# SyncE's first transfer becomes a small spare DMA transpose, and the x rows come as one transfer from ScalarE's queue

## The chip, the cores and the metric

The kernel runs on one core of a Trainium2 chip. The metric is the device time of one execution in microseconds. Before the change six executions gave a median of 272.99 us (272.6 to 274.35); at prediction time three of them were known, with a median of 272.78. A profile's span leaves out about 2 us at the ends (271.2 of 273.31 us in the profiled run before), so spans and times are not mixed below.

## The reference

```python
def reference(x, w_gate, w_up, w_down):          # x: 32 x 32 x 1024, bf16
    return (_gelu(x @ w_gate) * (x @ w_up)) @ w_down   # F = 3584, gelu by tanh
```

## The kernel before

A recorded program: each engine has its list of operations, and waits are worked out from the tiles that they share. Every transfer has a semaphore, and equal places in the schedule keep the order of the source. What matters here is the start. TensorE runs eight matmuls on constants, whose results are not used, transposes the first two column blocks of x itself, and the other blocks of x come by DMA transpose.

```python
        one = nc.const_aps.tensor(1.0, [P, 512], BF16)
        ...                                        # GpSimd builds the identity matrix
        for n in [512] * 6 + [P] * 2:
            mm(3, one[:, 0:P], one[:, 0:n], True, True)

        NX = 2
        for i, eng in enumerate(("sp", "act")):    # x rows, two halves, one on each queue
            dma(eng, xn[:, 2 * i:2 * i + 2, :], x_r[:, 2 * i:2 * i + 2, 0:NX * P], 0, f"xn{i}")

        def load_first(eng, j, k0, k1, after=()):  # j = 0: w_gate, 1: w_up
            dma(eng, first[:, j, k0:k1, :], w_r[j][:, k0:k1, 0:4 * P], 0, f"w0_{j}_{k0}", after)

        def load_x(h, k0, k1, after=()):
            pr.add("sp", "dma_start_transpose", xT[h][:, k0:k1, :], xf[h * 512:(h + 1) * 512, k0 * P:k1 * P],
                   dma=f"x{k0}_{h}", after=after)

        for k in range(NX):
            load_first("sp", 0, k, k + 1)
            load_first("act", 1, k, k + 1)
        for k0, k1 in ((2, 3), (3, 4), (4, 5), (5, 6), (6, 8)):
            load_x(0, k0, k1)
        for k in range(2, 4):
            load_first("act", 0, k, k + 1)
            load_first("act", 1, k, k + 1)
        act(warm[:, 0:1], const0, GELU, 0)
        for k in range(NX):
            for i, b in enumerate((6, 7) if k == 0 else (4, 5)):
                half = ps[:, b, 0:P].bitcast(BF16)
                for t in range(2):
                    pr.add("pe", "transpose", half[:, t * P:(t + 1) * P],
                           xn[:, 2 * i + t, k * P:(k + 1) * P], ident[:, :])
                pr.add("dve", "tensor_copy", xT[0][:, k, i * 256:(i + 1) * 256], half)
        ...
        # the first real matmuls: for k, for j (gate, up), for m in 0..3
        op = mm(2 * m + j, first[:, j, k, m * P:(m + 1) * P], xT[0][:, k, :], ...)
```

So the first real matmul needs three things: TensorE's transposes of the x rows, DVE's copies of them, and the first w_gate block. The destination tile of real matmuls is `arena` in the profile (`first` and `xT` lie in it); `xn` lies in `hT`.

Of the kernel before, what the change touches and what calls it, by code (L numbers as in the profile page):

```python
# [6 lines left out]
P = 128  # L7
# [116 lines left out]
def bass_standalone__geglu_ffn__sampling_kernel(  # L124
# [7 lines left out]
    xf = x.flatten_outer_dims()  # L132
# [3 lines left out]
    DK, FM = D // P, F // P  # L136
# [3 lines left out]
    x_r = xf.rearrange("(tc p) d -> p tc d", p=P)  # L140
# [3 lines left out]
    pr = _Program()  # L144

    with ExitStack() as es:
        def sb(name, shape, dtype):
            return es.enter_context(nc.sbuf_tensor(name, shape, dtype))

        hT = sb("hT", [P, FM, N], BF16)  # L150
# [15 lines left out]
        xn = hT[:, FM - 1, :].rearrange("p (t c) -> p t c", c=2 * P)  # L166
# [22 lines left out]
        def dma(eng, out, a, at, name, after=()):  # L189
            return pr.add(eng, "dma_start", out, a, at=at, dma=name, after=after)  # L190
# [10 lines left out]
            mm(3, one[:, 0:P], one[:, 0:n], True, True)  # L201

        NX = 2
        for i, eng in enumerate(("sp", "act")):
            dma(eng, xn[:, 2 * i:2 * i + 2, :], x_r[:, 2 * i:2 * i + 2, 0:NX * P], 0, f"xn{i}")

        def load_first(eng, j, k0, k1, after=()):
            dma(eng, first[:, j, k0:k1, :], w_r[j][:, k0:k1, 0:4 * P], 0, f"w0_{j}_{k0}", after)
# [414 lines left out]
```

## Time and profile before

| | before |
|---|---|
| median time | 272.99 us (6 runs, 272.6 to 274.35) |
| span of the profiled run | 271.2 us |
| TensorE busy | 267.6 us, 99% |
| x rows landed | 3.23 and 3.40 us |
| first w_gate block: issued, landed | 1.26, 4.25 us |
| first real matmul | 4.61 us |
| TensorE at full speed from | 6.3 us |

All places are microseconds from the start of the span. TensorE alone is the bound, so a later first matmul is paid at the end. The lines themselves are in the prediction below. Two of its habits are used throughout: start plus time to landing gives the landing, and the distance of two weight loads for 512 columns tells TensorE's speed: 0.43 us up to 6.3 us in this trace, called half speed below, and 0.216 us after it, called full speed.

### The profile page before, as it was taken

What the parts mean: (1) busy time and instruction counts of PE and PEld (TensorE: products, weight loads), DVE (VectorE), ACT (ScalarE), POOL (GpSimd) and SP (SyncE); (2) the same over time, 40 slices, a digit from 0 to 9 for tenths busy, and PEclk for the clock granted to TensorE, in tenths of its full rate; (3) what the DMA queues carried; (4) which work ended last, traced back from release to release, by engine and by line L of the source; (5) the groups of instructions that cost most, each with busy time, mean ns of one, the idle gap of its engine ahead of it and who ended that gap; (6) DMA issues with size and microseconds to landing.
All of it is one profiled execution on the core that took longest, in us unless ns stands there. A gap on an engine that the chain in (4) does not pass through costs nothing.

```text
span 271.2 us, 3314 instructions
## 1 busy us (share of the span) xinstructions
PE 267.6 (99%) x1197; PEld 191.8 (71%) x1206; DVE 203.5 (75%) x238; ACT 132.8 (49%) x213; POOL 37.2 (14%) x23
## 2 busy tenths in 40 slices
PE   8999999999999999999999999999999999999996
PEld 4444448888888888888776776664458888888884
DVE  1341998998899889988764739289976999999911
ACT  2335776566756675667455564531220305067452
POOL 1000003023302330234345060000000000000000
PEclk9999999999999999999999999999999999999999
DMA  7999960050492500942900070293010000002102
GB/s 189 275 282 186 276 187 4 9 147 0 120 294 53 155 0 2 282 145 65 248 0 0 0 259 14 81 347 117 0 39 19 4 0 0 0 0 80 58 19 97
DMA packets 47039, 27.46 MB, mean 101 GB/s; under 512 B 8624, under 2 KB 47024, under 8 KB 47024
## 3 DMA queue, kind: packets, MB, share of 16 engines
q1 hardware_dynamic: 44800, 25.30, 34.4%
q10 hardware_dynamic: 2224, 1.97, 2.8%
q8 instruction: 9, 0.15, 0.2%
q14 instruction: 6, 0.05, 0.1%
HBM read 23.33 MB, written 2.10 MB: 94 GB/s over the span
## 4 chain that ended last, share of the span: by engine, by line
PE 99%; issue 0%; DVE 0%
PE ps L117 99%; DVE o L117 0%
## 5 line engine op out<-in xcount | busy, mean ns | idle before, releaser
L117 PE MATMUL ps<-S,T 128*128 128x512 f32 x560 | 129.2, 391 | 0.0
L117 PEld LDWEIGHTS ps<-S,T 128*128 128x128 f32 x560 | 105.1, 188 | 22.5
L117 ACT ACTIVATE tmp<-ps 128x512 f32<-128x512 f32 x64 | 38.0, 595 | 52.2 <-PE ps L117 52.2
L117 POOL TENSOR_TENSOR T<-arena 128x1024 fp32r<-128x1024 bf16 x17 | 36.5, 2156 | 124.4 <-PE ps L117 74.2
L117 PE MATMUL ps<-T,S 128*128 128x512 f32 x224 | 51.3, 390 | 0.0
L117 DVE TENSOR_TENSOR T<-arena,T 128x1024 fp32r<-128x1024 bf16 x42 | 50.9, 1218 | 0.2
L117 PEld LDWEIGHTS ps<-T,S 128*128 128x128 f32 x224 | 42.0, 188 | 8.8
L117 DVE TENSOR_TENSOR hT<-tmp,ps 128x512 bf16<-128x512 f32 x56 | 37.2, 684 | 14.3 <-PE ps L117 11.9
L117 ACT ACTIVATE ps<-ps 128x512 f32<-128x512 f32 x44 | 25.6, 583 | 36.6 <-PE ps L117 36.6
L117 PE MATMUL ps<-arena 128*128 128x512 bf16 x186 | 42.6, 384 | 0.4
L117 DVE TENSOR_TENSOR tmp<-ps,tmp 128x512 f32<-128x512 f32 x28 | 19.4, 692 | 23.2 <-PE ps L117 23.2
L117 PEld LDWEIGHTS ps<-arena 128*128 128x128 bf16 x192 | 17.8, 98 | 24.3 <-issue 3.2
L117 DVE TENSOR_TENSOR T<-arena 128x1024 fp32r<-128x1024 bf16 x25 | 30.0, 1220 | 5.0 <-PE ps L117 4.3
L117 DVE TENSOR_TENSOR ps<-ps,tmp 128x512 f32<-128x512 f32 x32 | 22.2, 695 | 3.0 <-PE ps L117 3.0
L117 PE MATMUL ps<-arena,hT 128*128 128x512 bf16 (+2 forms) x124 | 24.3, 355 | 0.1
L117 PEld LDWEIGHTS ps<-arena,hT 128*128 128x128 bf16 x126 | 11.7, 98 | 12.7 <-issue 0.5
L117 ACT ACTIVATE tmp<-tmp 128x512 f32<-128x512 f32 x28 | 17.6, 633 | 2.4 <-DVE tmp L117 2.1
L117 DVE TENSOR_TENSOR S<-hT 128x1024 fp32r<-128x1024 bf16 x14 | 16.6, 1219 | 0.0
L117 ACT ACTIVATE T<-arena 128x1024 fp32r<-128x1024 bf16 x14 | 14.8, 1059 | 0.0
L117 ACT ACTIVATE ps<-hT 128x512 f32<-128x512 f32 x18 | 10.7, 599 | 8.0 <-DVE hT L117 8.0
L117 ACT ACTIVATE hT<-ps 128x512 f32<-128x512 f32 x14 | 8.0, 599 | 10.8 <-PE ps L117 10.8
L117 PE MATMUL ps<-S 128*128 128x512 f32 x56 | 12.9, 389 | 0.0
(32 smaller groups left out, 89.1 us busy)
## 6 DMA issues: line engine op xcount, KB each, us to landing
arena<-in_w_down_dram SPq DMA_DIRECT2D x4, 1792.0 KB, 8.8
arena<-in_w_gate_dram SPq DMA_DIRECT2D x10, 512.0 KB, 4.0
arena<-in_w_up_dram SPq DMA_DIRECT2D x10, 512.0 KB, 5.4
out_dram<-arena SPq DMA_DIRECT2D x12, 128.0 KB, 1.7
arena<-in_w_gate_dram SPq DMA_DIRECT2D x4, 256.0 KB, 5.0
arena<-in_w_up_dram SPq DMA_DIRECT2D x4, 256.0 KB, 5.1
arena<-in_w_up_dram ACTq DMA_DIRECT2D x4, 128.0 KB, 4.0
arena<-in_w_gate_dram ACTq DMA_DIRECT2D x2, 256.0 KB, 4.0
```

The source lines that it names most:

```text
L117: ins = name(eng, *args, **kw) if callable(name) else getattr(eng, name)(*args, **kw)
```

## The change

Nothing states the intent. My reading is that the spare transpose was to pay for whatever a first DMA transpose costs before it matters, and that the x rows then had to leave SyncE's queue. The spare's destination is a piece of hT that is written over much later; its data are never used.

```diff
         NX = 2
-        for i, eng in enumerate(("sp", "act")):
-            dma(eng, xn[:, 2 * i:2 * i + 2, :], x_r[:, 2 * i:2 * i + 2, 0:NX * P], 0, f"xn{i}")
+        pr.add("sp", "dma_start_transpose", hT[:, FM - 2, 0:P], xf[0:P, 0:P], dma="spare")
+        dma("act", xn[:, :, :], x_r[:, 0:4, 0:NX * P], 0, "xn")
```

## The prediction

> **What bounds the kernel now.** I read the busy totals first, then the chain of work that ended last, then the timeline of the first 14 us, because the diff touches only the first transfers of two queues, and last the DMA rates of that stretch in half microseconds.
>
> The page's busy totals and its chain:
>
> ```profile
> PE 267.6 (99%) x1197; PEld 191.8 (71%) x1206; DVE 203.5 (75%) x238; ACT 132.8 (49%) x213; POOL 37.2 (14%) x23
> ...
> PE 99%; issue 0%; DVE 0%
> PE ps L117 99%; DVE o L117 0%
> ```
>
> TensorE is the bound from the first microsecond to the last, and nothing else carries more than a trace of the chain. The chain in order of time shows the one place that this change can reach:
>
> ```profile
> 0.73 0.04 issue
> 0.77 3.79 PE ps L117 x16
> 4.56 0.05 issue
> 4.61 8.11 PE ps L117 x33
> 12.72 0.05 issue
> ```
>
> Sixteen TensorE instructions run before 4.56 us: eight matmuls on constants that do no useful work, then eight transposes of x rows. The real stream begins at **4.61** and does not stop again for longer than 0.07 us. So a later start moves the end; an earlier landing of anything else buys nothing.
>
> The timeline (start, length, engine, operation, count, idle time before it and its releaser):
>
> ```profile
> 0.73 0.48 ACTq L117 DMA_DIRECT2D hT<-in_x_dram  x1
> ...
> 0.74 0.46 SPq L117 DMA_DIRECT2D hT<-in_x_dram  x1
> ...
> 0.77 2.93 PE L117 MATMUL ps<-const-bfloat16-1.0 128*128 128x512 bf16 x8 [0.77 <-PEq L608]
> ...
> 1.26 0.92 SPq L117 DMA_DIRECT2D arena<-in_w_gate_dram  x2
> ...
> 2.23 6.75 SPq L117 DMA_TRANSPOSE arena<-in_x_dram  x5
> ...
> 3.50 1.06 PE L117 MATMUL ps<-ident,hT 128*128 128x128 bf16 x8
> ...
> 3.96 0.93 DVE L117 COPY arena<-ps 128x256 bf16<-128x256 bf16 x4 [3.96 <-PE ps L117]
> ...
> 4.58 0.14 PEld L117 LDWEIGHTS ps<-arena 128*128 128x128 bf16 x2 [0.28 <-DMA arena<-in_w_gate_dram]
> 4.61 9.62 PE L117 MATMUL ps<-arena 128*128 128x512 bf16 x39
> 4.99 0.15 PEld L117 LDWEIGHTS ps<-arena 128*128 128x128 bf16 x1 [0.28 <-DVE arena L117]
> ...
> 5.84 0.15 PEld L117 LDWEIGHTS ps<-arena 128*128 128x128 bf16 x1 [0.28 <-issue]
> 6.27 7.25 PEld L117 LDWEIGHTS ps<-arena 128*128 128x128 bf16 x34 [0.28 <-issue]
> ```
>
> Three things are to be seen. The two halves of the x rows leave at 0.73 and 0.74; the answers on DMA issues give 2.7 and 2.5 us to landing, so 3.4 and 3.2. The transposes start at 3.50, just behind the constant matmuls, so those cover the wait. The first real matmul needs the DVE copies of the first column block (the second of the four ends near 4.46) and the first w_gate block (issued 1.26, landing 3.0 us later, 4.26). Both come together; that is the tuned start. Then the weight loads are 0.43 us apart up to 6.27, and afterwards 34 take 7.25 us, 0.216 apart: TensorE runs at half speed up to about 6.3 us.
>
> [...] 0.43 us then 0.216 us per matmul, the change at 6.3 us, 5.5 us after the first matmul. [...] with both queues filled, the rate is 283 to 326 GB/s and no higher:
>
> ```profile
> 1.50:2.00 0.50, 0.50 (x2) 0.15 (x1) 0.00 (x0) 0.00 (x0) 0.00 (x0) 1.00 0.13 41
> 2.00:2.50 0.50, 0.50 (x3) 0.22 (x2) 0.00 (x0) 0.00 (x0) 0.00 (x0) 1.00 0.95 283
> ...
> 3.00:3.50 0.50, 0.50 (x5) 0.23 (x3) 0.00 (x0) 0.00 (x0) 0.00 (x0) 1.00 1.09 317
> ```
>
> (The last two columns are the DMA engines' busy share and GB/s.) [...]
>
> **The change, part by part.**
>
> *Removed:* one 128 KB transfer from SyncE's queue (0.46 us of issue) and one wait of TensorE, since one semaphore now stands for both halves.
>
> *Moved:* ScalarE's first transfer carries 256 KB in place of 128. Its issue stays near 0.5 us: a later ordinary load of four 512-byte runs per partition took 0.51. First data came close to 1.9 us (41 GB/s in the half microsecond to 2.0, about 20 KB, under 0.1 us of full rate). 256 KB at 300 GB/s is 0.87 us, so the last byte is on its way at about 2.8. Before, the two halves shared the engines and held the same bytes: the same 2.8, then landings of 3.2 and 3.4. The gap from last byte to landing stays, so I expect **3.3 to 3.5** and transposes from 3.50 to 3.6. The third transpose waited for the second half; now the first waits for all, with 0.1 us less slack. Cost: 0 to 0.1 us.
>
> *Added:* one DMA transpose of one 128x128 block (32 KB). Of five transposes on this queue, the four of four blocks took 1.21 to 1.26 us of issue and the one of eight took 1.59. That is (1.59 - 1.26) / 4 = 0.08 us a block, so one block should take 1.26 - 3 x 0.08 = **1.0 us** of issue, an estimate from those rows. Its 32 KB are 0.1 us of the engines at 300 GB/s. Its destination, a piece of hT, is not used before 18 us.
>
> *Pushed back:* the first w_gate block leaves at about 0.74 + 1.0 + 0.05 = 1.8 instead of 1.26. Transfers issued at that place (1.76, 1.80) took 3.4 and 3.6 us to landing with both queues full; the one issued at 1.26 took 3.0. SyncE's queue now has 128 KB fewer in front of it and ScalarE's 128 KB more, so I take 3.1: landing at **4.9** instead of 4.26. The first real matmul, at 4.61, then starts near 4.9 to 5.0, 0.35 us later.
>
> *What this costs at the end:* while TensorE is at half speed, 0.35 us of delay is 0.35 / 0.43 = 0.8 matmul not done before 6.3 us. They are done later at 0.216 us each: 0.8 x 0.216 = **0.18 us**, provided that full speed still comes at 6.3.
>
> *What does not bite:* everything else on SyncE's queue is about 0.5 us later. Eight matmuls use one row block of x. With full speed from 6.27, the 17th matmul (block 2) starts at 6.27 + 12 x 0.216 = 8.9, the 25th at 10.6, the 33rd at 12.3. The transposed x blocks landed at 2.23 + 5.3 = 7.5, 3.48 + 6.1 = 9.6 and 4.78 + 5.0 = 9.8. The slacks are 1.4, 1.0 and 2.5 us, all over 0.5. The second w_gate block lands near 5.7 and is wanted at 7.1.
>
> Sum: +0.1 to +0.3 us on the middle case.
>
> **The rivals.**
>
> *A, the clock comes later.* TensorE's idle gap before the real stream grows from 0.25 us (4.36 to 4.61) to about 0.6. [...] For it: the three times before, 272.6, 272.78 and 274.35, already spread by 1.75[...]. [...] I give it about 15 to 20%; time 274 to 275.
>
> *B, the first transpose is dear.* The first of the five needed 5.3 us to landing although its issue was no longer than the others'. If a transpose holds up the ordinary transfers behind it on the same queue, w_gate lands at 5.5 to 6 and the start moves by 1 to 1.4 us, half of which counts at low clock: +0.5 to +0.7, and more of rival A. Against it: ordinary loads followed the later transposes (issued from 25.73) with a landing in 4.9 us, which is no worse than elsewhere. Time 273.5 to 274.5.
>
> *C, hidden or a small gain.* If w_gate lands by 4.5, the copies still set 4.61 and nothing moves: 272.8. A gain would need an earlier 4.61, and the copies stand in the way: constant matmuls until 3.5, transposes, copies, none of them shorter. A spare transpose that made the later ones faster would help blocks that already have 1.0 us of slack or more. So a gain beyond run-to-run luck is nearly excluded.
>
> **Range and chances.** The middle case is 272.78 + 0.2 = 273.0; with rivals A and B at their weights I put **273.1**. The low end, 272.4, is the best run before less its own scatter[...]. Two per cent is 5.5 us, more than the whole start-up stretch could lose short of a stall of the transposes: faster 0.01, same 0.97, slower 0.02.
>
> **What the changed profile would show.** Right: a first SyncE issue of about 1.0 us, w_gate's first issue at about 1.8 with some 3.1 us to landing, transposes on TensorE at 3.5 to 3.6, the first matmul on arena at 4.9 to 5.0 with the w_gate transfer as its releaser, matmul spacing changing at 6 to 7 us, and the chain after it unbroken as before. Wrong: an issue of the spare over 1.5 us, an arena matmul after 5.3, the spacing of 0.43 lasting past 8 us, or matmuls on blocks 2 and 3 that wait for an x transpose. If the x rows land after 3.8, the single transfer is the dearer part and my working of it failed.

## The result

The changed kernel is correct and takes **276.27 us** (median of 6 runs, 274.35 to 277.73) against 272.99. The ratio is 1.0107 (95% interval 1.0064 to 1.0150): slower by about 1.1%, inside the 2% that counts as the same, but outside the predicted 272.4 to 274.7. Ratios here and below are the mean time of one kernel's fast runs over that of the other's of the same rounds, so not quite the ratio of the medians.

The profiled run is the slowest of the six, 277.73 us with a span of 275.4; four of the others have spans of 274.0 and one of 272.0. So the profile shows the worst case, and its 4.2 us are more than the mean loss of about 3.

The busy totals and the chain on the page of the changed kernel:

```profile
PE 269.6 (98%) x1197; PEld 192.2 (70%) x1206; DVE 203.4 (74%) x238; ACT 132.8 (48%) x213; POOL 37.1 (13%) x23
...
PE ps L117 96%; DMA arena<-in_w_gate_dram 2%; SPq L117 0%; DVE o L117 0%
```

A DMA has come into the chain that was TensorE from end to end. Its beginning in order of time (start, length, what):

```profile
0.74 1.22 SPq L117
1.96 0.06 issue
2.02 4.94 DMA arena<-in_w_gate_dram
6.96 0.05 issue
7.01 9.92 PE ps L117 x33
```

The issue of the spare transpose takes 1.22 us of SyncE's queue, then the w_gate block needs **4.94 us** from issue to landing, and only then the real matmuls begin: 7.01 us instead of 4.61. The timeline tells what TensorE did meanwhile and afterwards:

```profile
0.73 0.42 ACTq L117 DMA_DIRECT2D hT<-in_x_dram  x1
...
3.77 0.77 PEld L117 LDWEIGHTS ps<-ident,hT 128*128 128x128 bf16 x8 [0.33 <-DMA hT<-in_x_dram]
...
7.00 0.13 PEld L117 LDWEIGHTS ps<-arena 128*128 128x128 bf16 x2 [2.47 <-DMA arena<-in_w_gate_dram]
...
12.10 0.15 PEld L117 LDWEIGHTS ps<-arena 128*128 128x128 bf16 x1 [0.28 <-issue]
12.45 5.28 PEld L117 LDWEIGHTS ps<-arena 128*128 128x128 bf16 x25 [0.20 <-issue]
```

The x rows came at 3.72, 0.3 us later than before; that is hidden behind w_gate. TensorE then stood still from 4.80 to 7.01. Its weight loads stay 0.43 us apart until 12.1: full speed comes at about 12.3 us, before it came at 6.3. The two losses add up to the whole. The start moved by 7.01 - 4.61 = 2.40 us. Half-speed work after the start lasts 12.3 - 7.01 = 5.3 us instead of 6.3 - 4.61 = 1.7, and each microsecond of it loses half (0.43 us a matmul against 0.216): (5.3 - 1.7) / 2 = 1.8. Together 4.2, and the spans differ by 275.4 - 271.2 = 4.2.

The DMA rates of the changed kernel (last column GB/s, before it the DMA engines' busy share):

```profile
3.00:3.50 0.50, 0.50 (x4) 0.17 (x2) 0.00 (x0) 0.00 (x0) 0.00 (x0) 1.00 1.14 326
3.50:4.00 0.50, 0.44 (x5) 0.23 (x4) 0.00 (x0) 0.00 (x0) 0.00 (x0) 1.00 0.94 74
4.00:4.50 0.50, 0.50 (x8) 0.50 (x6) 0.30 (x2) 0.16 (x1) 0.00 (x0) 1.00 0.33 41
4.50:5.00 0.50, 0.31 (x3) 0.04 (x1) 0.50 (x3) 0.50 (x1) 0.00 (x0) 1.00 0.68 133
5.00:5.50 0.50, 0.00 (x0) 0.00 (x0) 0.13 (x1) 0.50 (x1) 0.00 (x0) 1.00 0.99 301
```

The same two half microseconds from 3.5 in the kernel before:

```profile
3.50:4.00 0.50, 0.50 (x7) 0.50 (x6) 0.04 (x1) 0.00 (x0) 0.00 (x0) 1.00 0.93 279
4.00:4.50 0.50, 0.50 (x6) 0.29 (x3) 0.50 (x3) 0.27 (x1) 0.00 (x0) 1.00 0.96 326
```

Before, they moved 279 and 326 GB/s; here they move 74 and 41. ScalarE's queue is hit too: single packets of its second w_up block (issued at 1.74, 5.04 us to landing) are recorded with 0.71 to 0.98 us, where 0.046 is usual. The dip begins soon after the spare's last data packets (3.33) and outlasts its landing (4.39) a little. Theories to test: the spare transpose makes the dip; the merged rows do; the queue position does; and the idle gap, not the delay, costs the clock.

### The profile page after: what moved, and what is told of

It reads as the page before. It is cut to its first block, busy times and chain, and to the rows that moved or that the text cites.

```text
span 275.4 us, 3315 instructions
## 1 busy us (share of the span) xinstructions
PE 269.6 (98%) x1197; PEld 192.2 (70%) x1206; DVE 203.4 (74%) x238; ACT 132.8 (48%) x213; POOL 37.1 (13%) x23
## 4 chain that ended last, share of the span: by engine, by line
PE 96%; DMA 2%; SPq 0%; issue 0%; DVE 0%
PE ps L117 96%; DMA arena<-in_w_gate_dram 2%; SPq L117 0%; DVE o L117 0%
## 5 line engine op out<-in xcount | busy, mean ns | idle before, releaser
L117 PE MATMUL ps<-arena 128*128 128x512 bf16 x186 | 44.4, 396 | 2.6 <-DMA arena<-in_w_gate_dram 2.2
```

Of the source, the lines that this page charges most:

```text
L117: ins = name(eng, *args, **kw) if callable(name) else getattr(eng, name)(*args, **kw)
```

## The experiments

Twelve kernels ran. Apart from one that is wrong, all were correct. "Start" is the first real matmul.

### Taking the parts apart: merge_only, spare_plain, spare_halves

`merge_only` has the merged rows alone:

```diff
-        pr.add("sp", "dma_start_transpose", hT[:, FM - 2, 0:P], xf[0:P, 0:P], dma="spare")
         dma("act", xn[:, :, :], x_r[:, 0:4, 0:NX * P], 0, "xn")
```

> The x rows as one ScalarE transfer, no spare transpose: SyncE's first transfer is the w_gate block. Theory T (the spare transpose stalls the DMA engines for about 1 us after its packets): w_gate issued at 0.74, landing by 3.7; x rows landing at 3.3 to 3.7; first matmul on arena at 4.6 to 4.9; no half microsecond below 150 GB/s between 3.0 and 5.0 us; time 272.5 to 273.5. Rival M (the merged x transfer is what delays the start): x rows land at 3.7 or later and w_gate's landing after 5, first arena matmul after 5.5, time 275 or more.

Measured: ratio 1.0068 (1.0045 to 1.0091), median 274.87. My theory expected 273 and missed. w_gate landed at 3.58, but the rows at 4.47, and they now begin the chain:

```profile
0.74 3.73 DMA hT<-in_x_dram
4.47 0.04 issue
4.51 1.04 PE ps L117 x8
5.55 0.05 issue
5.60 9.01 PE ps L117 x33
```

In the packet records SyncE's w_gate packets begin at 1.8 us and the rows' packets only at 2.7; with the spare in front, the rows began at 1.8. Nearly no data move from 2.0 to 2.5 (45 GB/s), and no transpose has a packet by then. So this move has a cost of its own, and a dip can come without a transpose.

`spare_plain` keeps the changed order but makes the spare an ordinary transfer of the same block:

```diff
-        pr.add("sp", "dma_start_transpose", hT[:, FM - 2, 0:P], xf[0:P, 0:P], dma="spare")
+        dma("sp", hT[:, FM - 2, 0:P], xf[0:P, 0:P], 0, "spare")
```

> The changed kernel with the spare as an ordinary transfer of the same 128x128 block, same place and bytes. Theory T (it is the transposing that stalls): issue near 0.5 us, w_gate issued at about 1.3 and landing near 4.3, first arena matmul 4.6 to 5.0, no half microsecond under 150 GB/s from 3.0 to 5.0, time 272.7 to 273.7. Rival Q (anything in front of w_gate on SyncE's queue, with 256 KB in front on ScalarE's, delays it so): w_gate lands after 6, dip in the DMA rate between 3.5 and 4.5, time about 276.

Measured: ratio 1.0020 (0.9986 to 1.0055), median 273.54. Issue of the spare 0.40 us, w_gate issued at 1.21 and landed 3.09 us later, at 4.30; the rows at 3.94, start 5.07. Its DMA rates:

```profile
3.50:4.00 0.50, 0.22 (x3) 0.01 (x1) 0.00 (x0) 0.00 (x0) 0.00 (x0) 1.00 1.11 381
4.00:4.50 0.50, 0.50 (x6) 0.50 (x7) 0.08 (x1) 0.00 (x0) 0.00 (x0) 1.00 1.25 325
```

Where the transpose gave 74 and 41, the ordinary transfer gives 381 and 325. The start is 0.1 us late of the expected range, the rest is as the theory said. So here it is the transposing that delays w_gate (4.94 us to landing against 3.09), not the place in the queue. Its longer issue (1.22 us against 0.40) belongs to it: w_gate left 0.8 us earlier here, so this run does not part the issue from what follows it.

`spare_halves` adds the spare to the kernel before, between SyncE's half of the rows and w_gate:

```diff
             dma(eng, xn[:, 2 * i:2 * i + 2, :], x_r[:, 2 * i:2 * i + 2, 0:NX * P], 0, f"xn{i}")
+        pr.add("sp", "dma_start_transpose", hT[:, FM - 2, 0:P], xf[0:P, 0:P], dma="spare")
```

> The kernel before with only the spare transpose added, between SyncE's half of the x rows and w_gate. The x rows should land as before, 3.2 to 3.5. If the spare ahead of w_gate is the cause by itself: w_gate issued near 2.5, landing 6 to 7.3, first arena matmul after 6, time 275 to 277. If the spare hurts only together with the merged rows: w_gate lands before 5.5, first arena matmul before 5.6, time 273 to 274.

Measured: ratio 1.0110 (1.0064 to 1.0155), median 275.52. Rows at 3.40 and 3.59; the start at 6.56 follows w_gate, as expected of the spare as the cause by itself:

```profile
1.25 1.19 SPq L117
2.44 0.06 issue
2.50 4.01 DMA arena<-in_w_gate_dram
```

The spare alone costs as much as the whole change. The merged rows alone cost 0.7%, and on top of the spare nothing, because w_gate is later than the rows then. The two delays lie side by side and did not add: 1.0110 and 1.0068 alone, 1.0107 together.

### What the idle gap costs: after_fill, merge_fill

`after_fill` is the changed kernel with TensorE kept busy while it waits:

```diff
                 pr.add("dve", "tensor_copy", xT[0][:, k, i * 256:(i + 1) * 256], half)
+        for n in range(5):
+            mm(3, one[:, 0:P], one[:, :], True, True)
```

> The changed kernel with five more 512-column constant matmuls (5 x 0.43 = 2.1 us) between the transposes and the first arena matmul, so that TensorE is not idle from 4.8 to 7.0. Theory H (of the 4.2 us lost in the profile, 2.4 are the later start and the rest is that the clock stayed low until 12.2 us because of the idle gap): first arena matmul at 7.0 to 7.2 as before, spacing falls from 0.43 to 0.216 by 8 us, time 274.2 to 275.0. Rival (the gap does not matter to the clock): spacing changes near 12 us as in the changed kernel, time 276 or more.

Measured: ratio 1.0053 (1.0035 to 1.0071), median 274.52, all four runs within 0.7 us. Its weight loads:

```profile
4.49 0.25 PEld L117 LDWEIGHTS ps<-const-bfloat16-1.0 128*128 128x128 bf16 x2
...
5.88 0.15 PEld L117 LDWEIGHTS ps<-const-bfloat16-1.0 128*128 128x128 bf16 x1 [0.28 <-issue]
6.31 1.60 PEld L117 LDWEIGHTS ps<-arena 128*128 128x128 bf16 x8 [0.28 <-DMA arena<-in_w_gate_dram]
```

Work that is thrown away makes the kernel some 1.75 us faster than the changed one (276.27 - 274.52 of the medians; 1.5 by the two ratios): full speed is there at 6.3, just as the real matmuls begin. The start, 6.53, is earlier than expected, because w_gate took 4.26 us here with the same transfers in front of it; this landing varies from run to run. The two kernels ran in different rounds and the intervals of their ratios overlap slightly (from 1.0064 to 1.0071), but all four runs with the fill lie below five of the six without.

`merge_fill` does the same for the merged rows without the spare:

```diff
-        for n in [512] * 6 + [P] * 2:
+        for n in [512] * 8 + [P] * 2:
```

> The merged rows without the spare, with two more 512-column constant matmuls (0.85 us) that close the idle gap from 3.5 to 4.5 us. The rows landed at 4.47 and the first arena matmul stood at 5.6 without them, time 274.87, clock up only at 9.1 us. If the idle gap cost the clock: start still at 5.5 to 5.7, full speed by 7 us, time 273.2 to 273.9. If the later start is the whole cost: time 274.5 to 275.5.

Measured: ratio 1.0038 (1.0013 to 1.0063) against 1.0068 without the fill, median 273.88; start 5.44, at full speed, where `merge_only` reached it at 9.1. So by the ratios nearly half of what `merge_only` lost came through the clock; the intervals overlap, so the share is rough. It may be more: the filled kernel's chain has a new wait of 0.7 us near 12 us, for a later w_gate block.

The clock also fell again in two of the traces: in `spare_big` 0.50 was granted from 7.67 to 11.07, and this is the time by stretches of `spare_two` (both below), whose clock records change at 5.14, 8.56 and 11.97; after the busy times the third column from the end is the granted clock:

```profile
5.15:8.55 3.40, 1.34 (x7) 0.64 (x8) 0.00 (x0) 0.81 (x2) 0.00 (x0) 1.00 1.18 294
8.56:11.96 3.40, 3.40 (x10) 1.21 (x9) 0.00 (x0) 0.00 (x0) 0.00 (x0) 0.50 0.63 137
11.98:15.30 3.32, 3.32 (x17) 1.51 (x16) 0.58 (x1) 0.80 (x2) 0.00 (x0) 1.00 1.14 284
```

In the first stretch, 3.42 us from one record to the next, TensorE was busy for 1.34 us. The next one, of 3.41 us, was granted half the clock (0.50). That costs 1.7 us and makes the mean clock over a span of 274 us 0.994, both estimates from the 3.41 us at 0.50. Timed runs show such means: 0.993 or 0.994 in two of the six runs of the changed kernel and in the two longer ones of `spare_halves` (277.04 and 276.27, against 274.77 and 274.68 at 1.000). This figure does not show a late first rise: the profiled run of the changed kernel, at half speed until 12.3, is listed with 1.000, and its trace holds no clock record at all.

### Where the spare stands: spare_after_w, gate_act

`spare_after_w` issues the spare after the two w_gate blocks:

```diff
-        pr.add("sp", "dma_start_transpose", hT[:, FM - 2, 0:P], xf[0:P, 0:P], dma="spare")
...
             load_first("sp", 0, k, k + 1)
             load_first("act", 1, k, k + 1)
+        pr.add("sp", "dma_start_transpose", hT[:, FM - 2, 0:P], xf[0:P, 0:P], dma="spare")
```

> The spare transpose issued after the two w_gate blocks and before the x transposes. Theory T: the stall comes with it, later: a half microsecond under 150 GB/s about 0.6 us after the spare's packets, somewhere between 4 and 6 us, but w_gate's first block is in by 3.7, so the first arena matmul is at 4.6 to 4.9; later weight blocks may be waited for by up to 1 us; time 272.7 to 274. Rival O (the stall belongs to the first microseconds of the program, whatever is sent): the dip stays at 3.5 to 4.5 us.

Measured: ratio 1.0038 (0.9995 to 1.0080), median 273.56. w_gate landed at 3.62, the rows at 4.46 as in `merge_only`, start 5.46. The rate fell to 59 GB/s at 2.0 to 2.5 and never below 166 from 4 to 9 us. The time fits the theory, but the start is later than the expected 4.6 to 4.9, because the rows were late, and the expected dip after the spare did not come. So a transpose did not bring it in this trace.

`gate_act` moves w_gate's two blocks to ScalarE's queue:

```diff
         for k in range(NX):
-            load_first("sp", 0, k, k + 1)
+            load_first("act", 0, k, k + 1)
             load_first("act", 1, k, k + 1)
```

> The changed kernel with the two w_gate blocks moved to ScalarE's queue, ahead of the w_up blocks: nothing useful follows the spare on SyncE's queue before the x transposes. Theory P (w_gate was late because of its place behind the spare, in issue and in the stall): w_gate lands near 4.2, as w_up did there in the changed kernel, first arena matmul at 4.9 to 5.3, w_up near 6 to 6.8, time 273 to 274.3. Rival G (the stall holds every transfer, so the place does not matter): w_gate lands after 5.5, start after 5.7, time 275 or more.

Measured: ratio 1.0043 (1.0013 to 1.0073), median 274.18. Start 4.82, nearly the old one. w_gate landed at 4.77, later than the 4.2 expected, but not after 5.5. Here the loss comes later: TensorE's weight loads waited between 11 and 16 us for later blocks on ScalarE's longer queue.

```profile
PEld ps L117 <- DMA arena<-in_w_gate_dram: 1.0, 1, 1.0
PEld ps L117 <- DMA arena<-in_w_up_dram: 0.6, 1, 0.6
```

### What the spare does in the DMA engines: spare_alone, spare_two, spare_big, halves_act, plain_all

`spare_alone` lets the rows and w_gate wait until the spare has landed:

```diff
+        lone = pr.add("sp", "dma_start_transpose", hT[:, FM - 2, 0:P], xf[0:P, 0:P], dma="spare")
+        dma("act", xn[:, :, :], x_r[:, 0:4, 0:NX * P], 0, "xn", [lone])
...
+            load_first("sp", 0, k, k + 1, [lone])
```

> The changed kernel with the x rows and the w_gate blocks waiting for the spare's landing, so that the transpose runs with nothing else in flight. If the wait between a transpose's packets and its landing is its own (theory W[...]): it lands 3.3 to 3.7 us after issue as in the changed kernel (3.65), and afterwards no dip: w_gate then takes about 3 us to landing. If the long landing comes of sharing with the x rows' transfer (theory C): it lands 2.2 to 2.7 us after issue, an ordinary 128x128 block having taken 2.03. First arena matmul at 8 to 9 us either way; time 276 to 278.

Measured: with nothing else in flight the spare landed **2.31** us after its issue, against 3.65 in the changed kernel (the ordinary block of `spare_plain`, with others in flight, took 2.03), and w_gate afterwards needed 2.77. That fits theory C, sharing. The start, 7.80, was a little earlier than expected. But the rate dipped to 67 GB/s from 4.5 to 5.0, long after the spare had landed and before any other transpose had sent a packet.

`spare_two` puts a second spare behind the first (another block, its own semaphore), and `spare_big` takes four blocks in place of one (512 rows):

```diff
+        pr.add("sp", "dma_start_transpose", hT[:, FM - 2, P:2 * P], xf[0:P, P:2 * P], dma="spare2")
```

> The changed kernel with a second spare transpose (another 128x128 block) right behind the first. If each small transpose brings its own stall of the DMA engines (theory S): two dips below 100 GB/s, or one twice as long as the changed kernel's (about 1.0 us, 3.5 to 4.5), and w_gate lands at 8.5 or later. If only the change from transposing to ordinary transfers stalls once (theory B): one dip of about 1 us, w_gate later by its issue alone, near 7.6 (6.3 to 7.0 in the two profiles with one spare, plus about 1 us).

```diff
-        pr.add("sp", "dma_start_transpose", hT[:, FM - 2, 0:P], xf[0:P, 0:P], dma="spare")
+        pr.add("sp", "dma_start_transpose", hT[:, FM - 2, 0:512], xf[0:512, 0:P], dma="spare")
```

> The changed kernel with a spare of four blocks (512 rows, 128 KB) like the x transposes in place of one. Theory C with a cost for each colliding byte: the dip below 150 GB/s lasts 2 us or more, w_gate lands at 8 or later. Theory C with a cost for each collision: w_gate lands at 6.5 to 7.5, as with one block. Rival: a small transpose is the bad case and a full one streams, w_gate lands before 6.

Measured: with two, w_gate was issued at 3.27 and landed at 7.16, 3.89 later; the only half microsecond below 100 GB/s between 2 and 9 us was 4.5 to 5.0 (99). Two small transposes did not stall twice. With the big one, issue 1.23 us, w_gate landed 4.50 us after its issue at 6.53, with one dip to 139 on the way there. In these neither the number nor the size of what is transposed mattered much (3.89 and 4.50 us to landing, against 4.94 with one block); having one there did. (What else differs is said below the table of all looks.)

`halves_act` sends the rows as two transfers, both on ScalarE's queue, without a spare:

```diff
-        dma("act", xn[:, :, :], x_r[:, 0:4, 0:NX * P], 0, "xn")
+        for i in range(2):
+            dma("act", xn[:, 2 * i:2 * i + 2, :], x_r[:, 2 * i:2 * i + 2, 0:NX * P], 0, f"xn{i}")
```

> No spare; the x rows as two transfers of 128 KB, both on ScalarE's queue, w_gate first on SyncE's. In the run with the rows merged and no spare, they landed at 4.47 in place of 3.23 and 3.40. If the queue and its order did that (theory K): the second half lands at 4.3 to 4.6 here too, the first at about 3.8. If the merging did it (theory M2[...]): both halves are in by 3.7.

Measured: the halves landed at 3.62 and **5.97**, start 6.89. Merging is not what made the rows late here; the queue is. The second half was later than either theory said: SyncE's x transposes have packets from 3.5 us here, the earliest of all kernels, and the rate is 116, 110 and 83 GB/s in the three half microseconds from 4.0.

`plain_all` makes all early transposes ordinary transfers of the same rows, 256 bytes a run; its result is wrong:

```diff
-            pr.add("sp", "dma_start_transpose", xT[h][:, k0:k1, :], xf[h * 512:(h + 1) * 512, k0 * P:k1 * P], ...)
+            for k in range(k0, k1):
+                dma("sp", xT[h][:, k, :].rearrange("p (t c) -> p t c", c=P),
+                    x_r[:, 4 * h:4 * h + 4, k * P:(k + 1) * P], 0, f"x{k}_{h}", after)
```

> Wrong result on purpose: the changed kernel with the spare and all DMA transposes of the first half of x replaced by ordinary transfers of the same rows and bytes (256-byte runs). Theory C (a DMA transpose in flight together with ordinary transfers drops the total rate): no half microsecond below 200 GB/s from 2.5 to 9 us, w_gate's first block in by 4.4, the x blocks each 1 to 3 us earlier than the transposes' landings of 9.1 to 11.9. Rival F (the small 256-byte packets, not the transposing, cost the rate): dips to 100 to 200 GB/s between 4.5 and 8 us stay.

Measured: w_gate 3.01 us to landing, at 4.21, start 4.98. The rate still sagged to 183 GB/s at 4.5 to 5.0, so the expectation of no dip below 200 failed. From 5.5 to 9 us it averaged 288 GB/s, against 228 in `spare_plain`, whose x blocks are transposed. The x blocks gained little against that run: 7.75, 8.01, 9.03 and 10.26 for blocks 2 to 5, against 7.66, 9.06, 9.82 and 10.31. So the transposes slowed the mixture somewhat here, as far as one look each can tell, and neither of these two, without a transpose ahead of w_gate, has the deep dip.

### All looks side by side

How long the first w_gate block took to land went with what its queue had just ahead of it (us; from the records of issues and landings):

| kernel | ahead of w_gate on its queue | issued | issue to landing | start |
|---|---|---|---|---|
| before | half of the rows | 1.26 | 2.99 | 4.61 |
| spare_plain | ordinary block | 1.21 | 3.09 | 5.07 |
| plain_all | ordinary block | 1.20 | 3.01 | 4.98 |
| merge_only | nothing | 0.74 | 2.84 | 5.60 (rows) |
| merge_fill | nothing | 0.74 | 2.72 | 5.44 (rows) |
| spare_after_w | nothing | 0.74 | 2.87 | 5.46 (rows) |
| halves_act | nothing | 0.74 | 2.48 | 6.89 (rows) |
| spare_alone | transpose, already landed | 3.07 | 2.77 | 7.80 (rows) |
| gate_act | rows (ScalarE's queue) | 1.20 | 3.58 | 4.82 |
| changed kernel | transpose | 2.02 | 4.94 | 7.01 |
| after_fill | transpose | 2.01 | 4.26 | 6.53 |
| spare_big | transpose | 2.03 | 4.50 | 6.58 |
| spare_halves | rows, transpose | 2.50 | 4.01 | 6.56 |
| spare_two | two transposes | 3.27 | 3.89 | 7.21 |

One rival is not tested. Where a transpose is in flight ahead, w_gate also leaves later, into fuller queues, and in the kernel before, which has no spare, transfers took longer the later they were issued: 3.41 us at 1.76, 3.85 at 2.28, 4.53 at 2.76, 4.98 at 3.25. By that measure the landings of `spare_halves` and `spare_two` are no longer than usual for their time of issue; those of the changed kernel, `after_fill` and `spare_big` are. For the changed kernel the dip accounts for about 1.1 us, an estimate: from 3.5 to 5.0 it moved 124 KB where the kernel before moved 458, and the 334 KB are 1.1 us at 300 GB/s, a rate between the 279 and 326 that the kernel before showed from 3.5 to 4.5. No run sends an ordinary transfer from that place at 2.0 us.

## Why the prediction was wrong

**The bound and the place** were right: TensorE is the bound, only the first real matmul can move, w_gate is what it waits for, and the x blocks behind were never waited for.

**The issue of the spare** was put at 1.0 us from a slope of 0.08 us a block. It took 1.22, and `spare_big` with four blocks took 1.23: one block and four held the queue alike. That is 0.2 us.

**The rows** were put at 3.3 to 3.5 and landed at 3.72. It was hidden in the changed kernel, but the working was wrong: in `merge_only` and `halves_act`, with w_gate leading SyncE's queue, the rows came at 4.47 and 5.97. I had counted bytes on the engines, and the order in which the two queues' packets begin counted too (1.8 and 2.7 us in `merge_only`).

**The landing of w_gate is the step that failed.** The first matmul came at 7.01 instead of 4.9 to 5.0. "So I take 3.1: landing at 4.9" came from ordinary transfers under load, as if a transpose ahead were 32 KB more. It took 4.94 and landed at 6.96. `spare_plain` shows it: the same block in the same place as an ordinary transfer gives 3.09, almost the figure I had taken, though issued 0.8 us earlier. Rival B named this mechanism and then sized it too small, with w_gate at 5.5 to 6 instead of 6.96, on the evidence of transfers that followed a transpose at 25.7 us, when ScalarE's queue issued nothing. This transpose had both queues' transfers around it; that this made the difference is argued, not tested.

**The clock.** I took full speed at 6.3 us as given and put rival A at 15 to 20%, because the gap would be 0.6 us, up from 0.25; that weight, and with it the high end of 274.7, was an estimate of mine, and no trace at prediction time showed what a gap costs. By the ends on the chain the gap before was only 0.05 (4.56 to 4.61), and it became 2.2 us. Rival A then was about half of the loss, as `after_fill` shows: some 1.5 to 1.75 of about 3.3 us. The arithmetic of half cost at low clock was right; it holds the 4.2 us of the profiled pair together. The two terms were not independent: here the delay opened the idle gap of 2.2 us, and the clock penalty came with the gap (with it filled, full speed came at 6.3 us, not 12.3), so the chance of A should have been tied to that of B.

**What stays open.** Shown is that a spare transpose just ahead of w_gate makes it land 2.0 to 2.9 us later than in the kernel before (6.27 to 7.16 against 4.25), where an ordinary block in its place makes it 0.05 later, and that the transpose alone landed in 2.31 us. 0.75 us of this or more is w_gate's later departure. How much of the rest is the stall and how much only the later departure is not separated, and how the DMA engines lose the time is not shown. Dips to 45 to 67 GB/s came without any transpose too, soon after w_gate's first packets when that block led (`merge_only`, `spare_alone`), and `spare_after_w` had the transpose without the deep dip. The runs do not explain why the rate in the half microsecond from 2.0 us lay between 45 GB/s (`merge_only`) and 287 (`gate_act`), nor do they show how long a gap has to be to cost the clock. No experiment beat the kernel before, so no better version is offered.

## What to carry to other kernels

Before putting a transfer "that costs nothing" ahead of one that the bound engine waits for, look at what lands next on that queue. Here the cost was not the spare's 32 KB: its issue took 1.22 us (1.23 with four blocks), and the w_gate block behind it 4.94 us to landing, against 3.09 behind an ordinary block of the same size. When a delay opens an idle gap on TensorE in the first microseconds, look at the clock as well as the delay: discarded matmuls in the gap were worth 1.5 to 1.75 us here (`after_fill`). Two delays ahead of the same instruction did not add here (1.0110 and 1.0068 alone, 1.0107 together): test each alone and both together before putting a loss down to one.
